# An attention and two feed-forward layers in split fp32: the last weight matrix by seven products of sums instead of eight plain ones

## The chip, the cores and the metric

One core of one Trainium2 chip runs one program. The metric is device time in microseconds (us), the median of three runs. TensorE (PE in the profile, PEld for its weight loads) multiplies, VectorE (DVE), ScalarE (ACT) and GpSimd (POOL) prepare operands and empty the accumulators, SyncE (SP) issues nearly all DMAs.

## The reference, cut to what matters

```python
x = attention(q, k, v, w_pre, w_post)      # 4 batches of 448 tokens -> 1792 x 768
gate = 1 / (1 + exp(-(x @ w_gate)))        # w_gate, w_val: 768 x 1536, w_out: 1536 x 768
y = (gate * (x @ w_val)) @ w_out
h = y @ w2_in                              # w2_in: 768 x 2048
g = h * (1 / (1 + exp(-1.702 * h)))
out = g @ w2_out                           # w2_out: 2048 x 768
```

The weights arrive as float64, eight bytes an element.

## The kernel before, in words

**Precision.** Every fp32 operand of the feed-forward part is held as two fp32r tiles, a rounded `high` part (ACT copies it) and a `low` remainder (DVE subtracts). A product takes three matmuls: high by high, high by low, low by high. A weight piece (128 x 384) passes these steps, each a "unit" in one list: a DMA brings the float64 words to a `ws` buffer (`stage`), ACT takes one absolute value (`bits`), DVE builds the fp32 number in four steps (`conv1` to `conv4`), a DMA stores it to DRAM (`kept`), and if the piece is used at once, `high` (ACT) and `low` (DVE) split it into a `w` buffer. Pieces that are needed again are later read from `kept` and only split. `whole(i, False)` in the list is a piece that is converted and stored now and not used yet. There are five `ws`, five `wc` (conversion) and five `w` buffers. `ahead` emits the units up to four or five used pieces past the one that PE takes.

**Stages.** Tokens go in two blocks of 896. After attention, `run` calls `first(0)`, `first(1)`, `second(1)`, `second(0)`. In `first(0)` twelve pairs of plain products (`pg`, `pv`) make g, then `py` multiplies by w_out and the result goes to DRAM. In `first(1)` the products with w_gate and w_val run in `quarters`: a 2 x 2 scheme with seven products of sums (p = 1, 2, 6, 5, 7, 4, 3) instead of eight; then `py` again. `second(t)` makes h with `quarters` (`inner`, 126 matmuls of 448 columns per call) and then multiplies by w2_out. It works in two halves of the 2048 hidden rows: two calls of `inner` (252 matmuls), each result split at once by `hilo` into an `hx` tile; then for both column halves n and eight row pieces kc, seven token tiles of 128 rows times three matmuls of 384 columns (`po`), 336 matmuls per half. The first half's sums are copied to `kept` tiles in SBUF, the second half's are added on the way out.

**What sets the order.** The program is written in one order and each engine works through its own part of it in that order; there is no planner in this part. In the list of units 64 pieces of w2_in and w2_out are to be converted: 12 in `first(0)`'s `py`, 2 in `first(1)`'s products, 30 in `first(1)`'s `py`, and 20 (all of w2_out) in `second(1)`, where they are used at once.

## Time and profile before

| | us |
|---|---|
| median of 3 runs | 1414.53 (1412.51 to 1417.62) |
| the profiled execution | 1417.92 |
| its span, first to last instruction | 1415.9 |
| PE busy | 1393.1 (98%) |
| PEld busy | 1270.5 (90%) |
| DVE busy | 1040.9 (74%) |
| ACT busy | 798.5 (56%) |

The span is what the instructions cover; the execution's time has 2.0 us around it. The share of busy PE is not a peak rate, since a matmul's end overlaps the next; what a matmul costs is read from the length of a stretch of them, divided by their number. The clock granted to TensorE was 1.00 in every stretch that is shown, its upper level of 2.4 GHz.

### The profile page before, as it was taken

How to read it: one execution, taken by the hardware profiler on the slowest of the kernel's cores; microseconds unless marked ns; L12 is line 12 of the kernel's file. 1: busy time of each engine (PE TensorE's matmuls, PEld its weight loads, DVE VectorE, ACT ScalarE, POOL GpSimd, SP SyncE). 2: the span in 40 equal slices, each digit the busy share in tenths (PEclk: the TensorE clock that was granted, in tenths of full speed). 3: DMA queues.
4: the chain of work that ended last, by engine and by line, in shares of the span. 5: the costliest groups of instructions: out<-in, count | busy, mean ns of one | idle time of the engine just before them, and what ended most of it. 6: DMA issues, size and time to landing. Idle time of an engine off the chain costs nothing.

```text
span 1415.9 us, 25571 instructions
## 1 busy us (share of the span) xinstructions
PE 1393.1 (98%) x9120; PEld 1270.5 (90%) x9120; DVE 1040.9 (74%) x2438; ACT 798.5 (56%) x1839; POOL 168.3 (12%) x159
## 2 busy tenths in 40 slices
PE   7999999999999999999999999999999999999998
PEld 5888888888887999999999999899999999999998
DVE  6777677767869675778977878888974887843842
ACT  5877788777979433445445555345733744632631
POOL 2444344334320000000000000000000000000000
PEclk9999999999999999999999999999999999999999
DMA  6644534622436555458952223783252272221222
GB/s 159 186 141 135 158 114 139 178 95 97 159 117 208 165 169 166 147 170 270 293 178 75 62 68 92 258 286 106 79 166 66 71 256 79 72 74 34 68 62 74
DMA packets 188192, 194.37 MB, mean 137 GB/s; under 512 B 66956, under 2 KB 183968, under 8 KB 188064
## 3 DMA queue, kind: packets, MB, share of 16 engines
q1 hardware_dynamic: 187040, 192.49, 43.4%
q8 instruction: 72, 1.18, 0.4%
q14 instruction: 56, 0.46, 0.1%
q10 hardware_dynamic: 960, 0.23, 0.1%
q0 software_dynamic: 64, 0.01, 0.0%
HBM read 113.65 MB, written 40.50 MB: 109 GB/s over the span
## 4 chain that ended last, share of the span: by engine, by line
PE 88%; DVE 5%; ACT 2%; issue 2%; DMA 2%; POOL 1%; SPq 0%; DVEq 0%; POOLq 0%; ACTq 0%
PE pq L910 25%; PE po L1117 16%; PE py L863 11%; PE pso L326 8%; PE pg L863 6%; PE pv L863 6%; PE psv L345 4%; PE psp L281 4%; PE psq L241 4%; DMA gt<-sc 1%; DVE st L288 1%; PE pst L206 1%; ACT ex L295 1%; POOL ghl L274 1%; DVE at L210 1%
## 5 line engine op out<-in xcount | busy, mean ns | idle before, releaser
L910 PE MATMUL pq<-xy,w 128*128 128x448 f32 x1764 | 361.0, 366 | 0.0
L910 PEld LDWEIGHTS pq<-xy,w 128*128 128x128 f32 x1764 | 330.9, 188 | 29.1 <-DVE w L799 0.5
L1117 PE MATMUL po<-w,hx 128*128 128x384 f32 x1344 | 233.9, 336 | 0.2 <-DVE w L799 0.2
L1117 PEld LDWEIGHTS po<-w,hx 128*128 128x128 f32 x1344 | 232.9, 188 | 0.7 <-DVE w L799 0.5
L274 POOL TENSOR_TENSOR ghl<-gt,ghl 120x448 fp32r<-120x448 f32 (+1 forms) x143 | 163.6, 1148 | 240.8 <-ACT ghl L210 182.8
L326 PEld LDWEIGHTS pso<-w,ex 120*112 120x112 f32 (+1 forms) x1440 | 159.0, 177 | 24.5 <-ACT w L308 7.2
L863 PE MATMUL py<-g,w 128*128 128x448 f32 x864 | 175.3, 364 | 0.9 <-DVE g L892 0.9
L326 PE MATMUL pso<-w,ex 120*112 120x120 f32 (+1 forms) x1440 | 172.6, 270 | 3.6 <-ACT w L308 1.9
L863 PEld LDWEIGHTS py<-g,w 128*128 128x128 f32 x864 | 161.9, 187 | 14.0 <-DVE g L892 1.3
L281 PE MATMUL psp<-ghl,wphl 120*120 120x448 f32 x540 | 140.2, 385 | 2.5 <-ACT ex L295 1.7
L288 DVE TENSOR_REDUCE st<-psp 120x1 f32<-120x448 f32 x180 | 108.9, 614 | 33.1 <-PE psp L281 32.4
L799 DVE TENSOR_TENSOR w<-ws,w 128x384 fp32r<-128x384 f32 x152 | 83.4, 554 | 51.4 <-ACT w L793 48.7
L793 ACT CAST w<-ws 128x384 fp32r<-128x384 f32 x152 | 75.4, 508 | 75.9 <-PE po L1117 67.3
L295 ACT ACTIVATE ex<-psp,st 120x448 f32<-120x448 f32 x180 | 113.3, 635 | 8.5 <-DVE st L288 3.6
L732 ACT ACTIVATE wc<-ws 128x384 f32<-128x384 f32 x136 | 75.1, 555 | 58.5 <-DMA ws<-in_moe_w_in_dram 28.5
L281 PEld LDWEIGHTS psp<-ghl,wphl 120*120 120x120 f32 x540 | 88.6, 182 | 17.0 <-ACT ex L295 3.9
L793 ACT CAST w<-wc 128x384 fp32r<-128x384 f32 x92 | 47.2, 513 | 98.9 <-DVE wc L756 96.2
L863 PE MATMUL pg<-xy,w 128*128 128x448 f32 x432 | 91.5, 368 | 0.0
L863 PE MATMUL pv<-xy,w 128*128 128x448 f32 x432 | 91.2, 368 | 0.0
L863 PEld LDWEIGHTS pv<-xy,w 128*128 128x128 f32 x432 | 81.1, 188 | 8.2
L863 PEld LDWEIGHTS pg<-xy,w 128*128 128x128 f32 x432 | 80.9, 188 | 8.2
L210 ACT CAST ghl<-gt 120x448 fp32r<-120x448 f32 (+1 forms) x132 | 74.4, 570 | 16.6 <-PE psp L281 8.4
(92 smaller groups left out, 1853.4 us busy)
## 6 DMA issues: line engine op xcount, KB each, us to landing
gt<-sc SPq DMA_DIRECT2D x172, 210.0 KB
ws<-kept SPq DMA_DIRECT2D x90, 384.0 KB
kept<-wc SPq DMA_DIRECT2D x136, 192.0 KB
ws<-in_moe_w_out_dram SPq DMA_DIRECT2D x56, 384.0 KB
ws<-in_moe_w_in_dram SPq DMA_DIRECT2D x32, 384.0 KB
ws<-in_moe_w_gate_dram SPq DMA_DIRECT2D x24, 384.0 KB
ws<-in_moe_w_val_dram SPq DMA_DIRECT2D x24, 384.0 KB
nat<-in_k_dram SPq DMA_DIRECT2D x48, 112.0 KB
```

Of the source, the lines that this page charges most:

```text
L210: (eng.copy if eng is nc.scalar else eng.tensor_copy)(dst, src)
L274: eng.tensor_tensor(out=t[:m, 1], in0=gt.pop(s)[:m], in1=t[:m, 0].bitcast(F32), op=ALU.subtract)
L281: nc.tensor.matmul(ps[:m, :S], wphl[:m, wp, :m], t[:m, gp], start=(i == 0), stop=(i == 2))
L288: nc.vector.tensor_reduce(out=st[:m, 0:1], in_=pre[s][:m, :S], axis=AX.X, op=ALU.max, negate=True)
L295: nc.scalar.activation(t[:m], pre.pop(s)[:m, :S], AF.Exp, bias=st[:m, 0:1], scale=1.0, accum_out=st[:m, 1:2])
L326: nc.tensor.matmul(ps[:JC, c, :, :n], e[:m, c * JC:(c + 1) * JC], w[:m, :, :n], start=True, stop=True)
L732: self.nc.scalar.activation(c.bitcast(F32), self.staged[self.units[i][1]][:, :, 1].bitcast(F32), AF.Abs)
L793: self.nc.scalar.copy(w[:, 0], self.source(i))
L799: self.nc.vector.tensor_tensor(out=w[:, 1], in0=self.source(i), in1=w[:, 0].bitcast(F32), op=ALU.subtract)
L863: self.nc.tensor.matmul(acc[hb][:, :self.S], st, act[k0 + kc][hb][:, ap], start=(k0 + kc == 0 and part == 0 and ap == 0), stop=(k0 + kc == ...
L910: nc.tensor.matmul(x, st, A[p][c][:, ap], start=(first and c + part + ap == 0), stop=(c == self.KG - 1 and part == 1), skip_group_check=no ...
L1117: nc.tensor.matmul(po[tk][:, :PW], HX[kc][:, part, tk * 128:(tk + 1) * 128], w[:, wp], start=(kc == 0 and part == 0 and wp == 0), stop=(kc ...
```

## The change

In `second` the product with w2_out is written as a 2 x 2 scheme too: three of the seven token tiles (384 tokens) are one row half, three the other; the hidden rows kc < 8 and kc >= 8 are the other split, the two column halves n the third. Seven products of sums, each 8 kc x 3 tiles x 3 matmuls of 384 columns, replace eight; the seventh token tile is multiplied directly. All 16 hidden tiles of a block stay in SBUF as plain fp32 (`raw`); `form` makes the sums of activations and splits them, seven steps ahead of their use. PE accumulates in three banks U, three banks V and one for the direct tile; `keep` and `total` hold and add partial results.

The four sums of w2_out quarters are made once: for kc 0 to 3 beside the products of `first(1)`, for kc 4 beside its `py`, for kc 5 to 7 beside the first calls of `inner` in `second(1)` (`sums_out`, fed in small steps by `pump` after each product), split there, and stored split in DRAM (`sums2`). `second` reads them ready for PE into the `ws` and `w` buffers (`fetch`, up to nine pieces ahead); the plain quarters are read from `kept` and split in place (`halve`).

All 32 pieces of w2_out are converted early. The 64 conversions now stand: 30 among the plain products of `first(0)`, 12 in its `py` (as before in number), 3 in `first(1)`'s products, 19 in its `py`, none in `second`. The big activation tiles (`xy`, `gh`, `hx`, `kept`) now come from 45 equal blocks that are given back and taken again; `inner` no longer splits.

```diff
-        rest = [*range(o2, o3), *range(o3, o3 + 4), *range(o4, o4 + 4), *range(o4 + 2 * HK - 4, o4 + 2 * HK)]
+        rest = [*range(o3, len(self.pieces)), *range(o2, o3)]
         for i in range(o2):
             whole(i)
-            if i > o1 and i % 2:
+            if 6 <= i < o1 and (i % 3 or i in (12, 36)) or i > o1 and i % 2:
                 whole(rest.pop(0), False)
...
-            if j in (4, 8):
+            for _ in range(1 if j >= K1 - 6 else 0):
                 whole(rest.pop(0), False)
         for i in range(o1, o2, 2):
             kept_pair(i)
-            for j in range(0 if i in (o1, o2 - 2) else 3):
+            for _ in range(2):
...
+    def pump(self, ease=1.0):
+        if self.loads:
+            self.fetch()
+            self.halve()
+        if self.todo:
+            self.credit += self.rate * ease
+            while self.credit >= 1 and self.todo:
+                self.credit -= 1
+                self.todo.popleft()()
...
+    def sums_out(self, kcs, ring=3):
...
+        def put(kc, p, src, *after):
+            outs.rotate(1)
+            out = outs[0][:, :, :PW]
+            self.hilo(out, src)
+            self.after(1, lambda: nc.sync.dma_start(self.sums2[kc][p], out.bitcast(F32)))
+            for a in after:
+                self.tt(*a, ALU.subtract)
+
+        for kc in kcs:
+            yield lambda: None
+            yield lambda: None
+            yield lambda kc=kc: load(kc)
+            yield lambda: None
+            yield lambda: None
+            yield lambda: (self.tt(t1, b12, b11, ALU.subtract), self.tt(t2, b22, t1, ALU.subtract))
+            for p, src, *after in ((6, t2), (5, t1, (b11, b22, b12)), (7, b11, (t2, b21, t2)), (4, t2)):
+                yield lambda kc=kc, p=p, src=src, after=after: put(kc, p, src, *after)
...
         if t:
+            self.later_work(self.sums_out(range(4), 5), 55)
...
             self.A = self.next
+            self.later_work(self.sums_out(range(4, 5)), 17)
...
+    def fetch(self):
...
+        while self.fetched < len(seq) and self.fetched < self.used_up + 9:
...
+            if p in self.WHOLE:
+                n, half = self.WHOLE[p]
+                self.nc.sync.dma_start(w[:, 1].bitcast(F32), self.kept[self.o3 // 2 + 2 * kc + n][half])
+            else:
+                self.nc.sync.dma_start(w.bitcast(F32), self.sums2[kc][p])
...
+    def halve(self):
+        while self.halved < min(self.fetched, self.used_up + 5):
+            w = self.formed[self.halved]
+            if self.loads[0][self.halved][1] in self.WHOLE:
+                self.part(self.nc.scalar, w, 0)
+                self.after(0, lambda w=w: self.part(self.nc.vector, w, 1))
...
+    PHASES = (1, 2, 6, 5, 7, 3, 4)
...
+            if p == 6:
+                self.tt(x[:, b], x[:, b], y[:, b], ALU.add)
+                self.tt(x[:, a], x[:, b], x[:, a], ALU.subtract)
+            elif p == 7:
+                self.tt(x[:, b], y[:, b], x[:, a], ALU.subtract)
+            elif p == 3:
+                self.tt(y[:, a], y[:, a], x[:, a], ALU.subtract)
...
+        for f in range(4):
+            raw += [self.form(F32) for _ in range(4)]
+            last = f == 3
+            if f == 0 and t:
+                self.later_work(self.sums_out(range(5, HK), 5), 27)
+            elif f > 1:
+                self.rush()
+                self.later_work(work[:HK] if f == 2 else work[HK:], 12)
+            if last:
+                self.loads = (seq, False)
+            self.inner(raw[4 * f:], last)
...
+        for i, (p, kc) in enumerate(order):
+            acc = U if p in (1, 6, 7, 4) else V
+            w = weight()
+            x = H.pop((p, kc))
+            for tk in range(3):
+                matmuls(acc[tk], x[:, :, tk * 128:(tk + 1) * 128], w, kc == 0 and p in (1, 2, 5), kc == HK - 1)
+            self.give(x)
+            if p in (1, 2, 3):
+                matmuls(D_bank, rest_piece(kc + (0 if p == 1 else HK)), w, p == 1 and kc == 0,
+                        p != 1 and kc == HK - 1)
+            elif i in extra:
+                self.fetch()
+                matmuls(D_bank, rest_piece(extra[i]), weight(), extra[i] == 0, False)
...
+            self.flush(False)
+            self.fetch()
+            self.halve()
+            while forms < len(order) and forms < i + 7:
+                form(*order[forms])
+                forms += 1
...
+        for j in range(3):
+            copy_out(U[j], PW + j * 128, 0, nc.vector if j == 1 else nc.scalar)
```

TensorE, from the second block's `py` to the first `po`, in the kernel before (names as in the code; `hx` is the split hidden tile, `w` a split weight piece):

```order
L863 MATMUL py<-g,w 128x448 x432
L910 MATMUL pq<-xy,w 128x448 x252
L1117 MATMUL po<-w,hx 128x384 x336
L910 MATMUL pq<-xy,w 128x448 x252
L1117 MATMUL po<-w,hx 128x384 x336
```

and in the changed kernel (`xy` is any big block, `wf` a fetched weight piece):

```order
L875 MATMUL py<-xy,w 128x448 x432
L922 MATMUL pq<-xy,w 128x448 x504
L1303 MATMUL po<-wf,xy 128x384 x600
L922 MATMUL pq<-xy,w 128x448 x504
L1303 MATMUL po<-wf,xy 128x384 x600
```

A block's four calls of `inner` now stand together, and 600 matmuls of `po` follow where twice 336 stood.

VectorE among the plain products of `first(0)`, between two uses of `pv`, in the kernel before (each run of four rows is one weight piece's conversion):

```order
L886 TENSOR_TENSOR sg<-sg,pv 128x448 x2
L738 TENSOR_SCALAR wc<-wc 128x384
L750 SCALAR_TENSOR_TENSOR wc<-ws,wc 128x384
L744 TENSOR_SCALAR wc<-wc 128x384
L756 SCALAR_TENSOR_TENSOR wc<-ws,wc 128x384
L799 TENSOR_TENSOR w<-wc,w 128x384
L892 TENSOR_TENSOR g<-sg,g 128x448 x2
```

and in the changed kernel, one of the pairs with an added piece in the first place:

```order
L898 TENSOR_TENSOR sg<-sg,pv 128x448 x2
L750 TENSOR_SCALAR wc<-wc 128x384
L762 SCALAR_TENSOR_TENSOR wc<-ws,wc 128x384
L756 TENSOR_SCALAR wc<-wc 128x384
L768 SCALAR_TENSOR_TENSOR wc<-ws,wc 128x384
L750 TENSOR_SCALAR wc<-wc 128x384
L762 SCALAR_TENSOR_TENSOR wc<-ws,wc 128x384
L756 TENSOR_SCALAR wc<-wc 128x384
L768 SCALAR_TENSOR_TENSOR wc<-ws,wc 128x384
L811 TENSOR_TENSOR w<-wc,w 128x384
L904 TENSOR_TENSOR xy<-sg,xy 128x448 x2
```

A second conversion stands ahead of the split of the weight and of g.

VectorE in the second call of `inner` of `second(1)`, changed kernel (384 columns: `sums_out`; `w<-wt,w`: a weight's low part; `s<-s,pq` and `xy<-s,pq`: results of the call):

```order
L1036 TENSOR_TENSOR xy<-s,pq 128x448
L904 TENSOR_TENSOR xy<-xy 128x384
L1036 TENSOR_TENSOR xy<-xy 128x384
L811 TENSOR_TENSOR w<-wt,w 128x384
L904 TENSOR_TENSOR xy<-xy 128x384
L1036 TENSOR_TENSOR xy<-xy 128x384
L931 TENSOR_TENSOR s<-s,pq 128x448
L811 TENSOR_TENSOR w<-wt,w 128x384
L904 TENSOR_TENSOR xy<-xy 128x384
```

The rows of `sums_out` stand between the low parts that PE waits for.

## Rows read from the trace of the kernel before

**Rows 1.** The page: span, busy time, and the chain that ended last by engine.

```profile
span 1415.9 us, 25571 instructions
PE 1393.1 (98%) x9120; PEld 1270.5 (90%) x9120; DVE 1040.9 (74%) x2438; ACT 798.5 (56%) x1839; POOL 168.3 (12%) x159
PE 88%; DVE 5%; ACT 2%; issue 2%; DMA 2%; POOL 1%; SPq 0%; DVEq 0%; POOLq 0%; ACTq 0%
```

**Rows 2.** Stretches (start:end, length), one per stage; the columns stand in the first line.

```profile
core 0: us, PE busy (x) PEld busy (x) DVE busy (x) ACT busy (x) POOL busy (x), PEclk, DMA share, GB/s
458.00:641.00 183.00, 183.00 (x967) 166.28 (x966) 123.35 (x298) 73.13 (x148) 0.00 (x0) 1.00 0.54 165
641.00:728.00 87.00, 87.00 (x432) 80.66 (x431) 80.10 (x190) 41.78 (x87) 0.00 (x0) 1.00 0.85 278
728.00:882.00 154.00, 154.00 (x755) 141.14 (x754) 116.55 (x229) 81.02 (x171) 0.00 (x0) 1.00 0.24 73
```

**Rows 3.** What TensorE waited for from 458 us on: total, times, longest.

```profile
PE py L863 <- DVE g L892: 0.9, 1, 0.9
PE po L1117 <- DVE w L799: 0.2, 1, 0.2
```

**Rows 4.** The chain that ended last, in order of time: start, length, what, instructions.

```profile
469.99 7.44 PE pv L863 x36
...
641.11 87.36 PE py L863 x432
...
971.71 51.29 PE pq L910 x252
1023.00 58.24 PE po L1117 x336
...
1352.38 58.26 PE po L1117 x336
```

**Rows 5.** The end in order of time: start, length, engine, line, operation, tiles.

```profile
1409.42 1.21 PE L1117 MATMUL po<-w,hx 128*128 128x384 f32 x6
...
1410.14 0.48 ACT L1132 COPY ot<-po 128x384 f32<-128x384 f32 x1 [0.56 <-PE po L1117]
...
1411.13 1.49 DVE L967 TENSOR_TENSOR ot<-ot,kept 128x384 f32<-128x384 f32 x3
1411.71 1.33 SPq L1134 DMA_DIRECT2D out_dram<-ot  x3
```

**Rows 6.** VectorE without a gap, in order of time: the starts give each operation's cost.

```profile
884.85 0.35 DVE L738 TENSOR_SCALAR wc<-wc 128x384 f32<-128x384 f32 x1
885.12 0.55 DVE L750 SCALAR_TENSOR_TENSOR wc<-ws,wc 128x384 uint32<-128x384 uint32 x1
885.59 0.35 DVE L744 TENSOR_SCALAR wc<-wc 128x384 uint32<-128x384 uint32 x1
885.85 0.55 DVE L756 SCALAR_TENSOR_TENSOR wc<-ws,wc 128x384 uint32<-128x384 uint32 x1
886.32 0.56 DVE L799 TENSOR_TENSOR w<-ws,w 128x384 fp32r<-128x384 f32 x1
...
889.33 0.62 DVE L892 TENSOR_TENSOR g<-s,g 128x448 fp32r<-128x448 f32 x1
889.87 0.62 DVE L967 TENSOR_TENSOR s<-s 128x448 f32<-128x448 f32 x1
```

**Rows 7.** Short stretches with the busiest VectorE; columns as in rows 2.

```profile
655.70:670.20 14.50, 14.50 (x73) 13.44 (x72) 14.43 (x35) 9.06 (x20) 0.00 (x0) 1.00 0.86 283
...
997.60:1023.20 25.60, 25.60 (x129) 23.75 (x128) 23.53 (x47) 19.14 (x40) 0.00 (x0) 1.00 0.22 62
```

**Rows 8.** DMA from 645 to 655 us: all packets, and SP's queue with its share.

```profile
DMA packets 2686, 3.19 MB, mean 319 GB/s; under 512 B 189, under 2 KB 2686, under 8 KB 2686
q1 hardware_dynamic: 2686, 3.19, 97.7%
```

**Rows 9.** A weight load that ScalarE waited for, in order of time; columns as in rows 5.

```profile
886.87 0.96 SPq L723 DMA_DIRECT2D ws<-in_moe_w_in_dram  x2
...
890.57 0.55 ACT L732 ACTIVATE wc<-ws 128x384 f32<-128x384 f32 x1 [6.48 <-DMA ws<-in_moe_w_in_dram]
```

More of the change, by code (lines that the diff above doesn't have):

```diff
@@ L1 @@
 import itertools
+from collections import deque
 from contextlib import ExitStack
@@ L629, in __init__ @@
         assert not rest
-        for there in (early, range(len(self.pieces))):
-            second(0, there)
-            second(1, there)
+        self.ends = []
+        for t in range(2):
+            for f in range(0, K2, 4):
+                kept_sums([[o2 + 2 * (f + 2 * g + x) for x in range(2)] for g in range(2)])
+            self.ends.append((len(self.units) + 2, len(self.items)))
+            self.units += [("x", None, None)] * 3
+        self.limit, self.most = self.ends[0]
         self.want = set(self.used)
@@ L642, in __init__ @@
         self.turn = 0
+        self.blocks = deque()
+        self.places = 0
+        self.home = []
+        self.maker = None
+        self.credit = 0.0
+        self.loads = None
     def block(self, w, k0, nk, c0, nn):
@@ L659, in open, with room, form, give @@
         self.X = [[self.form() for _ in range(2)] for _ in range(self.KD)]
-    def form(self):
-        self.formed += 1
-        return self.xy_p[(self.formed - 1) % len(self.xy_p)].tile([128, 2, self.S], F32R, tag="xy", name="xy")
+    def room(self, n, **kw):
+        for _ in range(n):
+            self.places += 1
+            self.blocks.append(self.ctx.enter_context(self.tc.tile_pool(name=f"xy{self.places}", bufs=1, **kw)))
+    def form(self, dtype=F32R):
+        pool = self.blocks.popleft()
+        x = pool.tile([128, 2, self.S], dtype, tag="xy", name="xy")
+        self.home.append((x, pool))
+        return x
+    def give(self, *blocks):
+        for x in blocks:
+            i = next(i for i, (y, _) in enumerate(self.home) if y is x)
+            self.blocks.append(self.home.pop(i)[1])
+    def plain(self, block):
+        return block.rearrange("p a s -> p (a s)")
     def begin(self, work, due, left, stored):
@@ L809, in split @@
             self.once(f, i)
-        while (len(self.staged) < len(self.items) and
+        while (len(self.staged) < self.most and
                (len(self.staged) < self.NST or self.items[len(self.staged) - self.NST][2] <= k)):
@@ new lines, in fetch @@
+    def fetch(self):
+        seq, at = self.loads
+        while self.fetched < len(seq) and self.fetched < self.used_up + 9:
+            j = self.fetched
+            inw = j >= self.TAIL or j // 5 % 2
+            if inw:
+                mine = [i for i in range(j) if i >= self.TAIL or i // 5 % 2]
+                if not at or len(mine) >= 5 and mine[-5] >= self.used_up:
+                    break
+            else:
+                mine = [i for i in range(j) if i < self.TAIL and not i // 5 % 2]
+                if self.step < self.limit or len(mine) >= 5 and mine[-5] >= self.used_up:
+                    break
+            kc, p = seq[j]
+            pool, tag = (self.w_p, "w") if inw else (self.wst_p, "ws")
+            w = pool.tile([128, 2, self.PW], F32R, tag=tag, name="wf")
+            if p in self.WHOLE:
+                n, half = self.WHOLE[p]
+                self.nc.sync.dma_start(w[:, 1].bitcast(F32), self.kept[self.o3 // 2 + 2 * kc + n][half])
+            else:
+                self.nc.sync.dma_start(w.bitcast(F32), self.sums2[kc][p])
+            self.formed.append(w)
+            self.fetched += 1
```

268 lines of the change are left out of this document (179 added, 89 removed).

## The prediction

> **What bounds the kernel now.** I read the page first: PE is busy for 98% of the span and makes 88% of the chain that ended last [rows 1]. The reader should ask next where that holds. The stretches by stage show it: from 458 us on, PE fills every stage, while DVE stands at 67% in the plain products of `first(0)`, 92% in its `py` and 76% in the products of `first(1)` [rows 2]. From there to the end PE waited for another engine's data 1.1 us in all [rows 3]. The chain in order of time is then a row of stretches of matmuls [rows 4]. So behind 458 us the time is the number of matmuls times what one costs, plus the end. The first 458 us are attention, whose instructions are the same in both programs. A change behind it gains what it takes from PE, and loses what it makes PE wait.
>
> **What one matmul costs** comes from the stretches [rows 4]. 384 columns: (58.24 + 58.26) / 672 = 173.4 ns. 448 columns: 202.2 ns in `py` (87.36 / 432), 203.5 in `pq` (51.29 / 252), 206.7 in `pv` (7.44 / 36). Between these three the instruction is the same and the tiles differ.
>
> **The change part by part.**
>
> *Fewer matmuls.* A block's w2_out had 2 x 2 x 8 x 7 x 3 = 672 matmuls; now it has 7 x 8 x 3 x 3 = 504 for the products and 16 x 2 x 3 = 96 for the direct tile, 600 together. That is 72 less per block, 144 in all, of the same width: 144 x 173.4 ns = **25.0 us less**. The Trainium skill ("TensorE: Matmul & The Clock Gate", section "Wait — 56ns, not 53.3ns?") gives N / 2.4 + 2.5 ns from start to start, 162.5 ns for 384 columns, and so an estimate of 23.4 us. The rows contradict it here, in every width, and the sum stands on them.
>
> *The end.* PE ends at 1410.63; three DVE additions follow until 1412.62, the last DMA issue ends at 1413.04 and the span 2.86 us later [rows 1, 5]. Now only three tiles are emptied, two complete before PE ends. Behind the last matmul stand one ACT copy (0.48), one issue (1.33 / 3 = 0.44) and the same 2.86: 3.8 us against 5.3, **1.4 less**. If the store waits behind another in SP's queue, nothing is gained; if the issue overlaps the copy, 1.8.
>
> *Tiles at other addresses.* g, and part of the activations, move to the new blocks. If `py` went at `pv`'s cost it would lose 864 x 4.5 ns = 3.9 us; if all 1764 `pq` reached `py`'s cost, 2.3 would be won. Most of the new blocks stand where g and the second `xy` pool stood, so I take 0.
>
> *Conversions moved into `first(0)`.* DVE's costs are the distances between starts in a gapless piece [rows 6]: 0.27 us for conv1 or conv2, 0.47 for an operation on 384 columns, 0.54 on 448. A conversion is 2 x 0.27 + 2 x 0.47 = 1.48, a `low` 0.47. A pair of plain products takes 2 x 7.44 = 14.88 us of PE and 4 x 1.95 + 4 x 0.54 = 10.0 of DVE, which is what the stretch shows (123.35 us over 12.3 pairs). 30 more conversions over 10.5 pairs add 4.2: 14.2 of 14.88, 95%. ACT adds 30 short operations to 73 us in 183, and DMA goes from 165 to about 262 GB/s (30 x 0.59 MB more). The added pieces stand ahead of used ones on ACT, DVE and in SP's queue, so a late load of one holds up the weight behind it. What covers this: weights are made four ahead, 4 x 3.72 = 14.9 us of PE. The nearest row is `py` of `first(0)`, with the same mixture: DVE was busy 14.43 of 14.50 us in one stretch, DMA at 283 GB/s, and PE did not wait [rows 3, 7]. I take 0. From above: if DVE also idles as it did in `py` (6.9 of 87 us [rows 2]), a pair takes 15.4 us, 0.5 too long, 5.6 over eleven pairs, hidden only as long as the four weights ahead last. Without cover the end of this row is **+5.6**.
>
> *`py`.* `first(0)`'s keeps its 12 conversions. `first(1)`'s has 19 for 30, 11 x 1.48 = 16.3 us less on DVE, and eight operations of `sums_out` (3.8) more. PE's 0.9 us wait for g stood here [rows 3]; the first column still has conversions ahead of g, so I leave it in.
>
> *The sums beside `first(1)`'s products.* Per kc: two loads, 8 DVE operations (3.8 us), 4 ACT copies, 4 stores. Four kc over the first four calls: 116.55 / 6 = 19.4 us of DVE per call [rows 2] becomes 23.2 of 25.8. The second call of `inner` before had 23.5 of 25.6 and PE did not wait [rows 3, 7]. Cost 0.
>
> *The calls of `inner` in `second(1)`.* Each loses eight lows of 448 columns (4.3 us of DVE). Three kc of sums bring 11.3 us, some 4.7 to each of the first two calls; the third call gets the remainder and eight forms (3.8). From 23.5 that makes 23.9, 23.9 and about 24.9 of 25.6 (counted from the order: 23.0, 24.4, 24.2). Here the lead is short: a weight's low part is issued two products ahead, 2 x 9 x 203.5 ns = 3.7 us, and at the start of the third call the work issued and not yet done comes to 4.0 by my count. I put **+0.5 to +1.5** here. In `second(0)` nothing is added, and DVE has 16 to 22 us per call.
>
> *The products.* PE spends 16.6 us on p = 1, 2 and 3 (96 matmuls), 14.6 on 5 and 7, 12.5 on 6 and 4. The fullest for DVE is p = 3 of `second(1)`: 32 operations, 15.8 us of 16.6 (the splits for p = 4, the halves, three `total` additions, the next block's sums); for ACT p = 7, 8.7 of 14.6. Operands are formed seven steps ahead, over 9 us. U and V are emptied while PE fills the other (12.5 us against three operations of 0.5). DMA is fullest in p = 5 of `second(1)`: 8 ready pieces (0.393 MB), 3 plain (0.197) and 4 activation loads (0.229) are 4.65 MB in 14.6 us, 319 GB/s, which is what the queue moved at 97.7% [rows 8]; p = 6 and 7 ask for 267 and 252. With five to nine pieces fetched ahead I take **+0.5**, at most 3.
>
> *Block edges.* Weights of p = 1 are fetched some five products before `inner` ends; three weights of the next `inner` are ready when p = 4 ends (5.5 us of PE), and the queue on ACT may wait for PE's release of a buffer there. Between 0 and 1 us each, three edges: **+0.5**.
>
> **Sum.** 1417.92 - 25.0 - 1.4 + 2.0 = 1393.5 for an execution like the profiled one. That one lay 3.4 us above the median of its runs, so the forecast is 1390.
>
> **The rivals.**
>
> *Weights come late in `first(0)`.* For it: 95% by count over 160 us, followed by a `py` that was at 92% already, so that no stage lets DVE catch up before 728 us. Against it: the stretch of 14.43 in 14.50 without a wait. 5.6 us in the products and up to as much again in `py`: 1396 to 1401.
>
> *The lead in `inner` and in `first(1)` is too short.* For it: the weights there are two products ahead only, and the added operations stand between the lows. Counted in this way the products of `first(1)` before come to 111.9 us, 4% under the stretch's 116.55 [rows 2]; at 10% under, the calls of 24.4 and 24.2 would take 26.7 of 25.6, and three calls of 23.5 0.3 too long each: 3 to 6 us with the waits for loads of sums: 1393 to 1396.
>
> *Slower than before: fetching doesn't keep ahead.* In `second` every step now needs a load of its own, 64 per block for 3 to 12 matmuls each, where before one of 32 pieces served 21 matmuls, 3.6 us. A load that ACT waited for took up to 3.7 us from issue to use [rows 9], a step lasts 1.56. If the lead falls below 2.4 steps, each piece is late by up to 2.1 us; twelve such pieces eat the 25 us, 13 make it slower, and a lead lost for one block would cost 64 x 2.1 = 134 us. It decides where `fetch` stands behind a store or a tile that isn't free in SP's queue. Against it: nine pieces, at least five buffers, 7.8 us. Time then: 1420 or more. The Trainium skill's fit in "DMA: Bandwidth & Descriptors" ("Anatomy of one DMA — SWDGE (gpsimd) path"), 2.0 us plus bytes / 436e3, gives an estimate of 2.9 us for such a load; with it the lead needed would be 1.9 steps.
>
> That the change does not do what it says is settled by the order: 600 matmuls stand where 672 stood, and the rest of PE's program is as long as before.
>
> **How the numbers follow.** Forecast, 1384 to 1395: 0.68. Late weights in `first(0)`: 0.14. Short lead: 0.11. Slower: 0.04; the remaining 0.03 are mixtures that end near the time before. The range goes from 1384 (no stall, 1.8 at the end, 2.3 from better addresses, and the spread of a median of runs that lie 2 to 3 us around it) to 1401 (the first rival whole). A measurement of this kernel can tell some 0.3% from no change, 4.2 us: faster means under 1410.3. That gives 0.93 faster, 0.04 the same, 0.03 slower.
>
> **What would show it.** In the changed kernel's trace: two `po` stretches of about 104 us (600 x 173.4 ns) each; no long wait of PE on a weight in 458 to 728 us, where DVE should stand near 95%; DVE over 90% in the first three calls of `inner`; a last store that ends under 4 us behind the last matmul. Wrong would be a `po` stretch above 107 us, PE waiting on `wf` or on a form, or on `w` in `first(0)`; and the forecast falls if the cost of a matmul of 384 columns isn't 173 ns.

## The result, and the profile after

The changed kernel takes **1396.72 us** (median of 4 runs, 1394.9 to 1400.11) against 1413.52 (1411.72 to 1417.62) for the kernel before on the same chip: a ratio of 0.988, 95% interval [0.9851, 0.9909]. It is faster by 16.8 us; 24 were forecast. The time lies inside the whole range given, 1384 to 1401, but 1.7 us above the band of the forecast itself (1384 to 1395). It stands where the prediction had put its first rival, late weights in `first(0)` (1396 to 1401), and the stages below show that this is not what happened: `first(0)` lost 1.1 us.

The profiled run of the changed kernel is its slowest (1400.11 us, span 1398.1). The page answers to [rows 1]: PE still fills 98% of a shorter span, with 144 matmuls less, and DVE rose from 74% to 80%.

```profile
span 1398.1 us, 26028 instructions
...
PE 1370.6 (98%) x8976; PEld 1247.2 (89%) x8976; DVE 1113.5 (80%) x2622; ACT 834.6 (60%) x1953; POOL 168.5 (12%) x159
```

The stretches by stage answer to [rows 2], with the stages of `second` added: plain products, `py`, products and `py` of `first`, then `inner` and products for each block. The columns are those of [rows 2].

```profile
456.80:639.40 182.60, 182.60 (x963) 165.87 (x962) 164.68 (x411) 86.79 (x173) 0.00 (x0) 1.00 0.80 252
639.40:727.90 88.50, 88.01 (x434) 80.78 (x433) 80.70 (x194) 44.15 (x93) 0.00 (x0) 1.00 0.89 295
727.90:884.00 156.10, 154.83 (x758) 141.66 (x757) 134.69 (x270) 87.99 (x187) 0.00 (x0) 1.00 0.43 132
884.00:976.00 92.00, 89.24 (x434) 82.27 (x433) 64.95 (x143) 33.86 (x73) 0.00 (x0) 0.98 0.65 214
976.00:1082.90 106.90, 104.06 (x505) 94.08 (x504) 94.45 (x193) 65.34 (x144) 0.00 (x0) 1.00 0.35 116
1082.90:1187.50 104.60, 104.60 (x602) 104.58 (x602) 81.88 (x170) 53.56 (x123) 0.00 (x0) 1.00 0.70 228
1187.50:1289.80 102.30, 102.30 (x505) 94.53 (x504) 80.18 (x164) 59.04 (x128) 0.00 (x0) 1.00 0.23 69
1289.80:1394.40 104.60, 104.59 (x601) 104.25 (x600) 61.58 (x132) 41.99 (x98) 0.00 (x0) 1.00 0.60 186
```

What PE waited for from 456.8 us on answers to [rows 3]: 7.4 us where it was 1.1. None of it is on `wf` or on a form, the new things in `second`.

```profile
PE pq L922 <- DVE w L811: 4.1, 6, 1.4
PE py L875 <- DVE xy L904: 2.8, 1, 2.8
PE py L875 <- DVE w L811: 0.5, 1, 0.5
```

**Where the difference went.** Stage lengths in us, from the first matmul of one stage to the first of the next, in the two profiled runs:

| stage | before | after | difference | forecast |
|---|---|---|---|---|
| attention (unchanged) | 458.3 | 456.8 | -1.5 | 0 |
| plain products, `first(0)` | 182.6 | 182.6 | 0 | 0 |
| `py`, `first(0)` | 87.4 | 88.5 | +1.1 | 0 |
| products, `first(1)` | 154.7 | 156.1 | +1.4 | 0 |
| `py`, `first(1)` | 88.6 | 92.0 | +3.4 | 0 |
| `inner`, `second(1)` | 102.6 | 107.0 | +4.4 | +0.5 to +1.5 |
| w2_out products, both blocks | 233.6 | 209.1 | -24.5 | -24.0 (-25.0, +0.5, +0.5) |
| `inner`, `second(0)` | 102.9 | 102.3 | -0.6 | 0 |
| behind the last matmul | 5.3 | 3.7 | -1.6 | -1.4 |

The sum is -17.9, the spans' difference -17.8. The saved work came out as forecast. The loss is in front of it: 10.3 us in four stages, where the sum held some 1.0. Attention, which the change does not touch, was 1.5 us shorter in this run; that is no gain of the change.

### The profile page after: what moved, and what is told of

Same layout as the page of the kernel before. It is cut to its first block, busy times and chain, and to the rows that moved or that the text cites. A ratio compares the mean times of both kernels' runs of the same rounds, so it can differ in the third digit from the quotient of the medians.

```text
span 1398.1 us, 26028 instructions
## 1 busy us (share of the span) xinstructions
PE 1370.6 (98%) x8976; PEld 1247.2 (89%) x8976; DVE 1113.5 (80%) x2622; ACT 834.6 (60%) x1953; POOL 168.5 (12%) x159
## 4 chain that ended last, share of the span: by engine, by line
PE 69%; DVE 16%; DMA 7%; ACT 4%; issue 3%; SPq 0%; POOL 0%; DVEq 0%; ACTq 0%; POOLq 0%
PE pq L922 21%; PE po L1303 15%; PE pso L327 9%; PE py L875 7%; PE psp L282 5%; PE psv L346 5%; PE psq L242 4%; DMA ws<-in_moe_w_out_dram 3%; DVE wc L762 3%; DVE wc L768 2%; DVE w L811 2%; DVE xy L904 2%; DVE wc L750 1%; PE pst L207 1%; ACT ex L296 1%
## 5 line engine op out<-in xcount | busy, mean ns | idle before, releaser
L1303 PE MATMUL po<-wf,xy 128*128 128x384 f32 x1200 | 209.3, 336 | 0.0
L1303 PEld LDWEIGHTS po<-wf,xy 128*128 128x128 f32 x1200 | 209.0, 188 | 0.1
L875 PE MATMUL py<-xy,w 128*128 128x448 f32 x864 | 177.5, 367 | 3.2 <-DVE xy L904 2.8
L327 PEld LDWEIGHTS pso<-w,ex 120*112 120x112 f32 (+1 forms) x1440 | 158.8, 177 | 24.5 <-issue 6.5
L875 PEld LDWEIGHTS py<-xy,w 128*128 128x128 f32 x864 | 163.0, 189 | 17.4 <-DVE xy L904 3.1
L289 DVE TENSOR_REDUCE st<-psp 120x1 f32<-120x448 f32 x180 | 108.8, 613 | 33.5 <-PE psp L282 32.8
L903 ACT CAST xy<-xy 128x384 fp32r<-128x384 f32 (+1 forms) x176 | 79.2, 473 | 47.6 <-DVE xy L1036 44.1
L904 DVE TENSOR_TENSOR xy<-xy 128x384 fp32r<-128x384 f32 (+1 forms) x176 | 85.1, 502 | 13.8 <-ACT xy L903 13.4
L805 ACT CAST w<-wc 128x384 fp32r<-128x384 f32 x72 | 36.8, 512 | 75.6 <-DVE wc L768 75.2
```

Of the source, the lines that this page charges most:

```text
L289: nc.vector.tensor_reduce(out=st[:m, 0:1], in_=pre[s][:m, :S], axis=AX.X, op=ALU.max, negate=True)
L327: nc.tensor.matmul(ps[:JC, c, :, :n], e[:m, c * JC:(c + 1) * JC], w[:m, :, :n], start=True, stop=True)
L875: self.nc.tensor.matmul(acc[hb][:, :self.S], st, act[k0 + kc][hb][:, ap], start=(k0 + kc == 0 and part == 0 and ap == 0), stop=(k0 + kc == ...
L903: self.nc.scalar.copy(dst[:, 0], src)
L904: self.after(n, lambda: self.nc.vector.tensor_tensor(out=dst[:, 1], in0=src, in1=dst[:, 0].bitcast(F32), op=ALU.subtract))
L1303: nc.tensor.matmul(acc[:, :PW], x[:, part], w[:, wp], start=(start and part == 0 and wp == 0), stop=(stop and part == 1), skip_group_check ...
```

## Experiments

All runs lie beside runs of the kernel before on one chip; the medians of before were 1413.3 to 1416.8. The table has the stages that moved (us, one profiled run each) and the median. "Plain" is the plain products of `first(0)`, "products" those of `first(1)`, "inner" the first `inner` stretch.

| kernel | plain | py of first(0) | products | py of first(1) | inner | median | ratio to before |
|---|---|---|---|---|---|---|---|
| changed kernel | 182.6 | 88.5 | 156.1 | 92.0 | 107.0 | 1396.72 | 0.988 |
| e1 no sums in inner | 182.6 | 88.1 | 156.6 | 91.3 | 102.8 | 1396.48 | 0.987 |
| e2 no early pieces in py | 179.2 | 88.9 | 155.6 | 87.4 | 106.1 | 1392.46 | 0.984 |
| e3 no early conversions | 179.2 | 87.4 | 156.1 | 92.6 | 107.4 | 1394.68 | 0.9867 |
| e4 other addresses | 179.8 | 88.9 | 156.0 | 90.8 | 106.7 | 1396.85 | 0.988 |
| e5 sums earlier | 180.1 | 89.3 | 156.0 | 122.7 | 102.7 | 1425.05 | 1.0072 |
| e6 subtract on GpSimd | 179.2 | 89.4 | 156.6 | 87.4 | 111.6 | 1398.76 | 0.9889 |
| e7 more conversions | 195.4 | 90.6 | 156.1 | 90.0 | 107.3 | 1416.09 | 0.9999 |
| e8 sums on GpSimd's queue | 179.2 | 88.5 | 155.7 | 87.4 | 108.8 | 1395.06 | 0.9883 |
| e9 = e5 and e8's queue | 181.0 | 88.6 | 155.5 | 96.4 | 102.7 | 1399.69 | 0.9895 |
| e10 loads earlier | 182.6 | 87.4 | 156.0 | 87.4 | 104.2 | **1391.54** | 0.9822 |
| e11 = e10 and e8's queue | 179.3 | 89.4 | 155.8 | 87.4 | 105.3 | 1392.83 | 0.9837 |
| e12 = e9 and e10's loads | 179.7 | 89.8 | 156.2 | 96.5 | 102.7 | 1399.14 | 0.9876 |

The column "plain" has two paces that the edits do not explain (last section), which shifts a total by up to 3.4 us, and attention, the same in all, took 455.8 to 460.6 us. So a stage is read from its own length and the median only for larger differences.

### e1: the sums beside `inner` left out

```diff
-                self.nc.sync.dma_start(w.bitcast(F32), self.sums2[kc][p])
+                self.nc.sync.dma_start(w.bitcast(F32), self.sums2[kc % 5][p])
...
-            if f == 0 and t:
-                self.later_work(self.sums_out(range(5, HK), 5), 27)
-            elif f > 1:
+            if f > 1:
```

> Left out: the sums of weights for kc 5 to 7, which the changed kernel makes beside the first calls of inner in second(1); the products read those of kc 0 to 2 in their place (the output isn't the reference's). Theory: the 24 added VectorE operations and their loads and stores in SP's queue make the low parts of the weights late there; without them the four calls take 102 to 103 us instead of 106.9, TensorE waits under 0.5 us for w in them (2.8 before), and the median falls by about 4 us to 1392.5. Rival: the forms, the plain tiles or the shared blocks make inner late; then the four calls stay above 105.5 us and the median within 1.5 us of 1396.7.

The stretch went from 107.0 to 102.8 us and PE waited for nothing in it: the whole loss there is the sums'. In the changed kernel the rows of three engines show the chain of it. SP stands 6.33 us in four stores of sums that DVE has still to make, and the next load of quarters goes out behind them; DVE then waits for that load; then PE waits for weights, `w`, behind DVE. In order of time, SP, then DVE, then PE, of the changed kernel:

```profile
1008.41 6.33 SPq L1018 DMA_DIRECT2D sb<-xy  x4
1014.78 1.21 SPq L1012 DMA_DIRECT2D xy<-kept  x2
...
1019.65 1.62 DVE L1036 TENSOR_TENSOR xy<-xy 128x384 f32<-128x384 f32 x3 [2.11 <-DMA xy<-kept]
...
1021.79 2.08 PE L922 MATMUL pq<-xy,w 128*128 128x448 f32 x9 [0.36 <-DVE w L811]
1025.30 9.68 PE L922 MATMUL pq<-xy,w 128*128 128x448 f32 x45 [1.42 <-DVE w L811]
```

The total did not fall with the stage: 1396.48, where 1392.5 was expected. Runs of a kernel differ by as much, so this run alone does not show that it would.

### e2: no pieces converted at the start of `py`

```diff
-            for _ in range(2):
+            for _ in range(2 if i > o1 + 2 else 0):
                 if rest:
```

> One order changed: in py of first(1) no piece is converted beside the first two weight pairs, and the 19 follow two by two after them. Theory: ScalarE and VectorE stand behind late loads of float64 pieces there while the last g waits behind them; without them TensorE's wait of 2.8 us for g falls below 0.5, its clock stays at the upper level through the first column, the stage takes 88 us instead of 92.0 and the median falls by about 3.5 us to 1393. Rival: VectorE is late from the products before, with the sums; then the wait for g stays above 2 us and the median within 1 us of 1396.7.

`py` of `first(1)` fell from 92.0 to 87.4 us and runs as one piece, without a wait:

```profile
882.29 87.56 PE L875 MATMUL py<-xy,w 128*128 128x448 f32 x432
```

In the changed kernel PE waited once there, for the last activations (the g of [rows 3], now `xy`), and its granted clock fell to the lower level behind it. Its row in order of time:

```profile
900.65 75.47 PE L875 MATMUL py<-xy,w 128*128 128x448 f32 x364 [2.76 <-DVE xy L904]
```

The stretches behind it, in the columns of [rows 2] (the clock is the third from the end):

```profile
900.70:902.00 1.30, 1.30 (x5) 1.18 (x6) 0.99 (x3) 0.00 (x0) 0.00 (x0) 0.66 0.99 264
902.00:904.00 2.00, 2.00 (x7) 1.80 (x6) 0.51 (x2) 1.09 (x3) 0.00 (x0) 0.50 1.04 369
904.00:906.00 2.00, 2.00 (x10) 1.82 (x10) 1.99 (x5) 1.19 (x3) 0.00 (x0) 0.87 0.40 136
906.00:908.00 2.00, 2.00 (x12) 1.85 (x11) 1.90 (x4) 0.84 (x2) 0.00 (x0) 1.00 0.84 200
```

2.76 of wait and 1.3 x 0.34 + 2 x 0.50 + 2 x 0.13 = 1.7 of lower clock are 4.5; 4.6 came back. The median fell by 4.3 us, but this profiled run was also 3.4 us shorter in the plain products, so it is the stage's length and not the median that shows the effect.

Why was g late? In both kernels the conversions in front of it wait for their loads of w_in on ACT. The same stretch, from the first matmul of `py` until g is there, in the kernel before:

```profile
882.90:897.80 14.90, 13.99 (x70) 12.62 (x68) 13.59 (x32) 4.04 (x9) 0.00 (x0) 1.00 0.71 223
```

and in the changed kernel:

```profile
884.00:900.60 16.60, 13.90 (x69) 12.55 (x67) 14.44 (x34) 6.33 (x13) 0.00 (x0) 1.00 0.74 240
```

DVE did two operations more (0.85 us) and idled 0.85 longer: 1.7 of the 1.8 by which the wait grew. The old order had no piece to convert behind the first pair of `py`; the new one has two behind each.

### e3: the conversions in `first(0)` left out

```diff
-        rest = [*range(o3, len(self.pieces)), *range(o2, o3)]
+        rest = [*range(len(self.pieces) - 2, len(self.pieces)), *range(o2, o3)]
...
-            if 6 <= i < o1 and (i % 3 or i in (12, 36)) or i > o1 and i % 2:
+            if i > o1 and i % 2:
...
```

> Left out: the conversion of 30 pieces of w2_out beside the plain products of first(0); pieces of w_gate that are already stored are read in their place (the output isn't the reference's). Theory, as predicted: these conversions cost TensorE nothing; first(0) stays at 270 to 271 us (271.0 with them), VectorE's share in the plain products falls from 90% to 67%, and the median stays within 1.5 us of 1396.7. Rival of the prediction: weights come late there; then first(0) falls below 268 us and the median below 1393.5.

`py` of `first(0)` came out at 87.4 us for 88.5. That is the price of the 30 conversions: 1.1 us here, and 0 to 2.4 over the other kernels that have them (87.4 to 89.8). The plain products were at 179.2 us, but so they were in e2, e6 and e8 with all 30, so that is not theirs. It is also why `first(0)` came to 266.6 us, under the 268 that the rival named; the median, 1394.68, fell into the band of neither.

### e4: the same program, all later tiles moved in SBUF

```diff
-    pad.tile([128, 8], F32, name="pad")
+    pad.tile([128, 24], F32, name="pad")
```

> One size changed: an unused tile at the upper end of SBUF is 64 bytes per partition longer, so that the first thirteen big blocks, the w and ws buffers start 64 bytes lower, on a multiple of 128 bytes as the 32 new blocks do. Theory: the moving operand's address is what parts the 206.7 ns of pv from the 202.2 ns of py; then pv goes to 202 ns, the calls of inner to 202 to 203 (204.6 now), and if 384 columns do likewise po from 174.2 to about 170; together 3.9 + 4 + 4.8, the median falls to 1384 to 1389. Rival: the order of tiles or the accumulating banks part them; then every cost stays and the median is within 1.5 us of 1396.7.

The total stayed. The w2_out products gained 0.5 and 0.4 us (104.0 and 104.2), and `inner` of `second(0)` lost 1.8 (104.2). `pv` went to 202.6 ns a matmul, as the theory said, but e2, e3, e6 and e8 have that pace with the tiles unmoved. So in this run the addresses moved a matmul by 1 to 4 ns, in either direction, and none of the lost time came back by them.

### e5: all sums of chunks 4 to 7 in `py` of `first(1)` (with e2)

```diff
-            self.later_work(self.sums_out(range(4, 5)), 17)
+            self.later_work(self.sums_out(range(4, 8), 5), 17)
...
-            if f == 0 and t:
-                self.later_work(self.sums_out(range(5, HK), 5), 27)
-            elif f > 1:
+            if f > 1:
```

> Full computation. Two things against the changed kernel: py of first(1) no longer begins with early pieces (as in e2_no_early_pieces_in_py, 1392.46 us), and the sums of chunks 5 to 7 are made in py of first(1), with those of chunk 4, and none in the first calls of inner. Theory: the 4.3 us that the first inner stretch lost are the subtractions beside its own sums and conversions and the loads behind SyncE's stores, and py of first(1) has room on VectorE (65 of 87 us busy, 76 with these sums). Then the first inner stretch is 102.5 to 103 us (107.0 in the changed kernel), py of first(1) 87.4 to 89, and the median 1388 to 1390. Rival: py of first(1) can't take them, since its transfers rise from 214 to about 300 GB/s beside late loads of w_in; then that stretch is 91.5 us or more and the median no better than 1392.5.

The first `inner` stretch is at 102.7, as expected, but `py` takes 122.7 us and the kernel is slower than before the change: ratio 1.0072 [1.0057, 1.0087]. DVE was busy 76.06 us of these 122.7, so it had no lack of time. What PE and DVE waited for in that `py` and behind it:

```profile
PE py L875 <- DVE w L811: 25.8, 5, 9.0
...
DVE xy L1036 <- DMA xy<-kept: 41.1, 4, 11.3
```

SP in order of time, then DVE:

```profile
940.60 2.17 SPq L1018 DMA_DIRECT2D sb<-xy  x3
942.82 2.49 SPq L1012 DMA_DIRECT2D xy<-kept  x2
954.64 0.33 SPq L771 DMA_DIRECT2D kept<-wc  x1
...
950.86 1.15 DVE L1036 TENSOR_TENSOR xy<-xy 128x384 f32<-128x384 f32 x2 [11.19 <-DMA xy<-kept]
```

DVE stood from 939.7 to 950.9 for quarters whose load SP issued at 942.82, behind stores of sums and of pieces. Behind DVE stood the weights and also the conversion that SP's next store waited for (954.64): two queues in order that wait for each other's next entry in turn.

### e6: the subtractions of the sums on GpSimd (with e2)

```diff
-            self.hilo(out, src)
+            nc.scalar.copy(out[:, 0], src)
+            self.after(0, lambda: self.gp(out[:, 1], src, out[:, 0].bitcast(F32)))
...
-                self.tt(*a, ALU.subtract)
+                self.gp(*a)
...
```

> Full computation. As e2_no_early_pieces_in_py, and every subtraction that makes the sums of w2_out and their low halves runs on GpSimd, which is idle from 458 us on, and no longer on VectorE; order and places stay. Theory: it is VectorE's share of the sums (24 of 26 us busy per call) that makes TensorE wait for w beside first(1)'s products and in the first inner stretch; with 4 to 5 us less per call the waits go, the products of first(1) take 154.7 us (156.1), the first inner stretch 102.3 to 103 (107.0), and the median is 1387 to 1389. Rival: the stores wait for GpSimd, which is slower for each subtraction, and SyncE, which stands in those stores, issues the loads behind them as late as before or later; then the first inner stretch stays at 106 us or more and the median at 1392 or more.

The rival came true: `inner` took 111.6 us. DVE got emptier (87.0 us busy for 94.2 in e2), yet PE waited up to 4.11 us, since ACT, which makes the high half of each sum and also the weights', stood for GpSimd. GpSimd in turn stood 5.52 us for a load of quarters, which SP issued at 1008.38 behind four stores of sums that had kept it for 6.98 us: the chain of e1 again, with slower subtractions in it. A row of POOL, one of ACT and one of PE, in order of time:

```profile
1013.31 7.84 POOL L1037 TENSOR_TENSOR xy<-xy 128x384 f32<-128x384 f32 x8 [5.52 <-DMA xy<-kept]
1015.45 0.93 ACT L1017 CAST xy<-xy 128x384 fp32r<-128x384 f32 x2 [5.18 <-POOL xy L1037]
...
1021.62 59.46 PE L922 MATMUL pq<-xy,w 128*128 128x448 f32 x277 [4.11 <-DVE w L811]
```

### e7: twelve conversions more in `first(0)`

```diff
+            elif 6 <= i < o1:
+                whole(o3 + i // 3 - 2, False)
```

> Full computation, with 12 conversions done twice: the changed kernel's 30 conversions beside the plain products of first(0) become 42, the 12 extra ones repeat pieces and change no result. Theory: the change is near the edge there (VectorE 164.5 of 182.4 us busy, 90%), so that the cover of the 30 is gone with 12 more: 12 x 2 x 0.45 us or more on VectorE bring it to 96 to 100%, and the stretch of plain products and py behind it get longer by 4 to 11 us together, the median 1401 to 1408. Rival: the four weights held ready and the share left over cover that too; then the two stretches stay within 2 us of the changed kernel's and the median within 1394 to 1399.

The theory held, at a higher price: the plain products took 195.4 us for 182.6, `py` 90.6 for 88.5, and the whole gain of the change was gone (1416.09, ratio 0.9999). The stretch in the columns of [rows 2]:

```profile
456.40:651.90 195.50, 188.23 (x964) 163.22 (x963) 181.03 (x454) 92.24 (x184) 0.00 (x0) 1.00 0.85 270
```

What PE waited for, in the plain products and `py`:

```profile
PE pv L877 <- ACT w L807: 2.7, 6, 0.7
PE pv L877 <- DVE w L813: 2.4, 8, 0.6
PE pg L877 <- DVE w L813: 1.8, 7, 0.3
```

PE in order of time, at the same place of two pairs in a row:

```profile
551.61 6.77 PE L877 MATMUL pg<-xy,w 128*128 128x448 f32 x32 [0.26 <-DVE w L813]
...
568.53 6.75 PE L877 MATMUL pg<-xy,w 128*128 128x448 f32 x32 [0.26 <-DVE w L813]
```

A pair took 16.9 us, where the count gives DVE 10.0 + 4 x 1.48 = 15.9 (it was busy 16.0). Add the same 6% to the changed kernel's count of 14.2 and it comes to 15.1 of 14.9. By this estimate its 30 conversions stand right at the edge.

### e8: the sums' loads and stores on GpSimd's queue (with e2)

```diff
-                nc.sync.dma_start(d, self.kept[...])
+                nc.gpsimd.dma_start(d, self.kept[...])
-            self.after(1, lambda: nc.sync.dma_start(self.sums2[kc][p], ...))
+            self.after(1, lambda: nc.gpsimd.dma_start(self.sums2[kc][p], ...))
```

> Full computation. As e2_no_early_pieces_in_py (1392.46 us, first inner stretch 106.1), but the loads and stores of the sums of w2_out are issued on GpSimd's queue, which is empty there, and no longer on SyncE's; what VectorE and ScalarE do, and in which order, stays. Theory 1, the queue: SyncE stands in the sums' stores until VectorE has made them, the loads behind them go out late, and VectorE and then TensorE wait for those. Then the waits on w go, the first inner stretch is 102.5 to 103.5 us, the products of first(1) lose their waits (154.7 to 155), and the median is 1388 to 1389.5. Theory 2, the share: VectorE at 22 to 24 of 26 us is what makes w late, whoever issues the transfers; then the first inner stretch stays at 105.5 us or more and the median at 1391.5 to 1393.

Neither theory: `inner` got longer, 108.8 us. The load stood behind the sums' own stores in the new queue too, so the edit did not take it from behind them, and DVE waited 3.46 us for it, instead of 2.0. From its issue to DVE's first use it took 5.9 us, where e2 on SP's queue had 4.7. POOL, then DVE, in order of time:

```profile
1005.67 0.69 POOL L1018 DMA_DIRECT2D sb<-xy  x1 [1.78 <-DVE xy L904]
1006.24 1.57 POOL L1012 DMA_DIRECT2D xy<-kept  x2
...
1012.18 1.62 DVE L1036 TENSOR_TENSOR xy<-xy 128x384 f32<-128x384 f32 x3 [3.46 <-DMA xy<-kept]
```

The load starts when the last sum of the chunk before is stored, and is wanted some two steps later. That lead was too short in both queues.

### e9: e5 with the sums' transfers on GpSimd's queue

> Full computation. As e5_sums_earlier (sums of chunks 4 to 7 all in py of first(1), none in the first calls of inner; 1425.05 us, that py 122.8 us with 27 us of TensorE waiting for w), but with the loads and stores of the sums on GpSimd's queue. Theory: those 35 us are a ring of two queues in order: VectorE stood four times, 41 us in all, for a load of a sum's quarters that SyncE had not issued, since SyncE stood in a store of a piece that VectorE had still to make. With the sums' transfers out of SyncE's queue VectorE never waits so; then py of first(1) is back at 87.4 to 91 us, the first inner stretch at 102.5 to 103, and the median at 1387 to 1392. Rival: it is the transfers' rate (late loads of w_in beside 4 chunks of sums) that fails there; then py stays over 100 us and the median over 1402.

`py` fell from 122.7 to 96.4 us, between the numbers of the two theories: the ring of the two queues was 26 of the 35 us. 9 stayed; DVE still waited 12.5 us for loads, in three pieces of 4.1 to 4.2.

### e10: the next chunk's quarters loaded earlier (with e2, on SP's queue)

```diff
             for a in after:
                 self.tt(*a, ALU.subtract)
+            if p == 7 and kc != kcs[-1]:
+                self.after(0, lambda: load(kc + 1))
...
-            yield lambda kc=kc: load(kc)
+            yield lambda kc=kc: load(kc) if kc == kcs[0] else None
```

> Full computation. As e2_no_early_pieces_in_py (1392.46 us, first inner stretch 106.1), but the quarters of each next chunk of the sums are loaded when the third sum of the chunk before is made, some six steps ahead of their first use and no longer two; all on SyncE's queue, sums at the same steps. Theory: the lead of the load is what the first inner stretch lacks (VectorE stood 2 to 3.5 us for it there, with and without SyncE's stores ahead of it). Then VectorE waits 0 to 0.5 us for these loads, the first inner stretch is 102.5 to 103.5 us, and the median 1388 to 1389.5. Rival, the share: VectorE at 22 to 24 of 26 us is too full beside four forms a call whatever its loads do; then the waits for loads go, but TensorE's waits for w stay, the stretch at 105 us or more, and the median at 1391 to 1393.

DVE no longer waits for a load of quarters, and `inner` takes 104.2 us for 106.1. PE's waits there are down to 0.5 us, and the weight loads' to 2.0 (3.9 in e2). It did not reach 103.5. The stretch of e10, in the columns of [rows 2]:

```profile
970.90:1075.10 104.20, 103.67 (x505) 94.17 (x504) 94.40 (x193) 65.34 (x144) 0.00 (x0) 1.00 0.37 119
```

and that of e1, which has no sums:

```profile
976.80:1079.60 102.80, 102.80 (x506) 94.59 (x505) 83.37 (x169) 60.71 (x132) 0.00 (x0) 1.00 0.20 59
```

So both theories have a part: the loads' lead 1.8 us, DVE's share 1.4 to 1.9. For the second speaks that every wait left in e10's stretch is for a low half from DVE, and that e1 has none; an edit that changes DVE's share alone was not run. This version has the lowest median, 1391.54 us (1391.02 to 1392.17), ratio 0.9822 [0.9808, 0.9837]. It beats both kernels; its lead on e2 (0.984 [0.9826, 0.9855]) is not clear of noise.

### e11 and e12: e10's loads with GpSimd's queue, and with e9

> Full computation. e10_loads_earlier with the sums' loads and stores on GpSimd's queue, as in e8_sums_on_gpsimd_queue (first inner stretch 108.8 us, median 1395.06). Theory of the lead: the first inner stretch is 102.5 to 103.5 us here too, the median 1388 to 1389.5; if e10 keeps a wait behind SyncE's stores and this one doesn't, the queue had its part. Rival, the share: 105 us or more, as in e10.

`inner` came out at 105.3 us, between the two numbers; no load of quarters is waited for, but DVE waited 1.3 us for plain pieces. The other queue brings nothing.

> Full computation. e9_earlier_and_queue (sums of chunks 4 to 7 in py of first(1), on GpSimd's queue; that py 96.4 us, median 1399.69) with the loads moved ahead as in e10. In e9 VectorE stood three times for the sums' loads, 4.2, 4.1 and 4.1 us, and TensorE 6.1 us for weights behind it. Theory of the lead: those waits go, py of first(1) is 87.4 to 89 us, the first inner stretch 102.7, and the median 1387 to 1389.5. Rival, the transfers (299 to 319 GB/s in the stretches with a chunk's sums, 0.95 of the DMA engines): the loads land late all the same; then py stays at 92 us or more and the median at 1393 or more.

The rival's numbers came: `py` stayed at 96.5 us. DVE's wait for quarters fell from 12.5 to 2.8 us, and ACT's for w_in rose from 4.3 to 13.7. What ACT waited for in this `py`:

```profile
ACT wc L744 <- DMA ws<-in_moe_w_in_dram: 13.7, 7, 3.8
```

A stretch of it with a chunk's sums, in the columns of [rows 2] (the last two are DMA share and GB/s):

```profile
900.00:910.00 10.00, 10.00 (x51) 9.26 (x51) 9.25 (x21) 4.23 (x9) 3.59 (x5) 1.00 0.94 321
```

One wait took another's place. That the transfers' rate is the reason is not shown: the next 10 us stand at 0.83, later ones between 0.44 and 0.94, and SP stood 54.4 us in this stage in stores of converted pieces that DVE had still to make, with loads of w_in behind them. The rate and the order of SP's queue were not tested apart. In either case the sums of chunks 5 to 7 are better placed beside `inner`, where DMA is at 0.35.

## Why the prediction was right, and which terms were mis-sized

**The number.** The forecast was 1390 and the median 1396.72. Its mechanism held: PE stayed the bound, the time fell by the matmuls taken away and rose by what PE was made to wait for. What failed is the price of those waits, put at some 1.0 us against 10.3 measured, in the terms `py` and the calls of `inner` above all.

**"Fewer matmuls": right; "The products" and "Block edges": right by luck.** 600 matmuls take 104.6 us, 174.3 ns each, for the 173.4 counted. The three terms together gave -24.0 and -24.5 came. But neither +0.5 was spent on late transfers or at the edges: PE waited for no form, for no `wf` and at no edge. What offset the 25.0 is the 0.9 ns more for each of 1200 matmuls, 1.1 us, for which the sum had no term. The Trainium skill's rule ("TensorE: Matmul & The Clock Gate", section "Wait — 56ns, not 53.3ns?"), which gives 162.5 ns, does not hold for these matmuls, after the change as before it; the measured row decides.

**"The end": right.** -1.6 for -1.4 (its own pieces, 5.3 less 3.8, give 1.5). The last copy of ACT starts with the last matmul's end; the span ends 3.7 us behind that. PE, SP and ACT in order of time:

```profile
1385.70 8.69 PE L1303 MATMUL po<-wf,xy 128*128 128x384 f32 x49
...
1393.89 1.43 SPq L1280 DMA_DIRECT2D out_dram<-ot  x3
...
1394.42 0.48 ACT L1298 COPY ot<-po 128x384 f32<-128x384 f32 x1 [0.56 <-PE po L1303]
```

**"Tiles at other addresses" at 0: right, its premise not.** e4 found -0.9 and +1.8 in single stages, and the same total. The prediction put the 206.7 ns of `pv` down to its tiles; with the same tiles `pv` took 206.7 ns in the changed kernel and 202.6 in e2, so the 3.9 us that it weighed are not shown to be a price of addresses.

**"Conversions moved into `first(0)`" at 0: nearly.** 1.1 us in e3, within 0 to 2.4. The row taken as nearest, DVE 14.43 of 14.50 without a wait [rows 7], pointed the right way, but e7 shows how narrow it was: at four conversions a pair instead of under three, 15 us are lost.

**"`py`" of `first(1)` at 0: the largest miss in kind, +3.4.** The step that failed is "I leave it in": the wait of 0.9 was carried over unchanged, because the first column had conversions ahead of g before and after, and DVE's total there falls. The total was right and beside the point; the two conversions behind each of the first pairs decide, where the old order had none behind the first (e2). And the wait's price was more than its length here, since the clock fell behind it.

**"The calls of `inner`" at 0.5 to 1.5: the mechanism right, the size off, +4.4.** The sum counted DVE's time (about 24 of 25.6 a call, and so it was), which is worth 1.4 to 1.9 us (e10 against e1 and against 102.3). What was left out of the sum is the load of the next chunk, issued behind stores that wait for DVE; it is worth 1.8 (e2 to e10). Another 0.9 is gone in e2 (107.0 to 106.1); no run explains how. The rival "lead too short" named these loads and gave 1393 to 1396; it was nearer than the forecast. The same order of loads and stores, put where SP also serves conversions, costs 35 us (e5).

**"The sums beside `first(1)`'s products" at 0: +1.4, not settled.** PE waited 0.57 and 0.70 us there for `w`, behind three calls in which DVE was busy 23.5 to 24.2 of 26.0 us. All runs have 155.5 to 156.6 us. e6 and e8, which were to take these waits away, did not (156.6 and 155.7). A run without these sums was not tried, so that they are the cause is only argued.

**"Slower: fetching doesn't keep ahead": did not happen.** PE waited for no `wf`. The 2.9 us from the Trainium skill ("DMA: Bandwidth & Descriptors", "Anatomy of one DMA — SWDGE (gpsimd) path") belong to GpSimd's queue, while these loads go out on SP's, whose landings no run shows; on GpSimd's, beside `inner` in e8, loads of that size took 5.7 us (median).

## What to carry to other kernels

Work moved under a bound engine has to be counted in three queues, not one: the helper engine's time, the order of the transfers that feed it, and what stands behind both. A load issued behind a store that waits for the same engine has no lead of its own; issue it before the store, as soon as its buffer is free, and count it in steps until its first use. How many operations stand ahead of the one that the bound engine needs next matters more than their number in the whole stage.

## What the runs showed of the hardware

**A wait can cost more than its length, and need not.** Behind waits of 2.04, 2.76 and 3.40 us in `py` (e1, changed kernel, e3) the granted clock of PE fell to 0.50, the lower of its two levels, for some 3 us. Behind 0.94 (before), 1.42 (in `inner`) and 1.70 (e8) it stayed at 1.00, but so it did behind 2.38 (e7) and behind 2.76 in e4, as long a wait at the same place as in the changed kernel. So the wait's length alone does not decide. PE in e4, and the stretch behind, in the columns of [rows 2]:

```profile
898.08 74.03 PE L875 MATMUL py<-xy,w 128*128 128x448 f32 x364 [2.76 <-DVE xy L904]
...
900.00:902.00 2.00, 2.00 (x11) 1.85 (x10) 1.11 (x4) 1.69 (x4) 0.00 (x0) 1.00 1.04 373
```

**The plain products run at one of two paces.** 36 matmuls take 7.44 us (206.7 ns each) or 7.30 us (202.6), at a granted clock of 1.00, and the stretch 182.6 us (before, changed kernel, e1, e10) or 179.2 to 181.0 (the others but e7), in runs of programs that are the same up to there (e1, e2). The pace can change inside a run: e5, e9 and e12 begin at 7.30 and end at 7.44. In e5 it changes behind a wait of 0.25 us; e4 has one of 0.34 and keeps its pace. PE's rows in e5 in order of time (each holds another 0.16 us, the end of its last matmul):

```profile
606.89 7.46 PE L875 MATMUL pg<-xy,w 128*128 128x448 f32 x36
...
615.41 6.88 PE L875 MATMUL pv<-xy,w 128*128 128x448 f32 x32 [0.25 <-DVE w L811]
622.12 7.60 PE L875 MATMUL pg<-xy,w 128*128 128x448 f32 x36
```

What decides it is open; it is not the addresses alone (e4 moved them and is at 179.8, e2 is at 179.2 without).

**GpSimd beside DVE slows DVE.** In e6 a subtraction of 384 columns took 1156 ns on GpSimd, and DVE's own with two operands in SBUF rose from 550 to 629 ns on average (a weight's low part), the longest over 1.3 us, while those with an operand in PSUM stayed. Conversion steps with one operand rose as well where GpSimd was at work (five of them, up to 1.18 us for 0.35). DVE in order of time, in e6, with GpSimd at work from 1002.56 to 1007.78:

```profile
1004.25 1.36 DVE L779 TENSOR_TENSOR wt<-ws 128x384 f32<-128x384 f32 x1
1005.53 0.61 DVE L1040 TENSOR_TENSOR xy<-s,pq 128x448 f32<-128x448 f32 x1
...
1008.65 0.54 DVE L811 TENSOR_TENSOR w<-wt,w 128x384 fp32r<-128x384 f32 x1
```

The Trainium skill ("SBUF — State Buffer", section "SBUF: two separate sides") says that a VectorE operation with two SBUF inputs and a GpSimd operation that reads SBUF lock each other out of a shared pair of ports for a whole instruction; these rows agree as far as VectorE's side goes.
